# Moving the second probability tile of each attention step to GpSimd, in an attention and mixture-of-experts kernel

## The chip, the cores and the metric

The kernel runs on one core of one Trainium2 chip. The metric is the device time of one execution in microseconds (us). The five engines that matter here are TensorE (PE in the profile; PEld is its weight load), VectorE (DVE), ScalarE (ACT), GpSimd (POOL) and SyncE (SP), whose queue issues all DMAs of this kernel.

## The reference, cut to what matters

```python
scores = scale * np.matmul(q, k.transpose(0, 1, 3, 2))        # B=4, H=8, S=576, D=64
scores = scores + bias.transpose(2, 0, 1)[None]               # bias from a small MLP over positions
scores = scores - np.max(scores, axis=-1, keepdims=True)
attn = np.exp(scores)
attn = attn / (np.sum(attn, axis=-1, keepdims=True) + 1e-09)
x = np.matmul(attn, v)                                        # then (B*S, H*D) = (2304, 512)
...
for e in range(E):                                            # E=8 experts, F=1024
    out += P[:, e:e+1] * (np.maximum(x @ w1[e], 0.0) @ w2[e])
```

P comes from a Sinkhorn normalisation of the gate's softmax. All matrix products run in float16; where an operand needs more precision it is split into a float16 value (hi) and the float16 remainder (lo), and the products are summed.

## The kernel before

The program has two parts. The first (to about 490 us) computes the position bias, the attention, and as filler a large part of expert 0; the second runs the experts on what the attention left. The change touches the first part alone.

Work of the attention is cut by unit (16 units: a batch and a pair of heads) and step. A unit has five steps: four of two tiles (128 query rows x 576 keys each) and one of a single tile that holds the last 64 rows of both heads. That is 80 steps, 64 of them with two tiles, and 144 tiles. A step goes through these functions:

- `scores` (L897): PE writes the raw scores into one of two PSUM tiles `s`.
- `st_max` (L921): one custom VectorE instruction per tile adds the bias (tiles `br`, `br4`, `bt`), takes the row maximum into `st` and writes the result as float32 to `sb` (six buffers). The order listing calls it ISA, the profile CUSTOM_DVE_ANT_0.
- `st_exp` (L939): ScalarE takes the exponential in place in `sb`, with the row sum into `st`.
- `st_rcp` (L946): VectorE makes the reciprocal of the sum, a TENSOR_SCALAR and a RECIPROCAL on `st`.
- `st_hi` (L955): ScalarE multiplies `sb` by the reciprocal and rounds to float16, the first half of tile `ah` (two buffers; every third step in the middle units uses a part of `xc`).
- `st_lo` (L968): VectorE forms the remainder, `sb` times the reciprocal minus hi, as float16 in the second half of `ah` (SCALAR_TENSOR_TENSOR). Then one DMA, issued by SP, transposes the step's whole `ah` into `aT` (three buffers).
- `attend` (L982): PE multiplies `aT` by the split values `vs` into PSUM tile `pv`, two steps (LAG, L1105) after the step that completed the group.

Once per unit the queries and keys are split (`u_cut`, tile `qk`: ScalarE hi, VectorE lo), transposed on PE and copied out (`u_trans`, tile `qkT`), and the values split (`u_v`, tile `vs`). GpSimd has five copies per unit to do (`pairs`, L720: two of `qkT`, three of `vs`), and nothing else in this stretch apart from some copies of the bias.

From step 13 on, pieces of expert 0 (`run_piece`, L867; matmuls into tile `l`, evacuations to `area` and `ys`) are marked `later` and fill PE between the steps.

All of this is first recorded: class `Plan` holds each operation with its engine, a cost from `Engine.cost` (L226), and its dependencies, and `emit` (L130) replays it on a model of the engines and so fixes the order of every engine's queue, SP's included, before the kernel runs. Semaphores then enforce dependencies; each engine runs its own queue strictly in order. The line of nearly all instructions of this part is therefore that of the recorder, L210, and they are told apart by their tiles.

Of the kernel before, what the change touches and what calls it, by code (L numbers as in the profile page):

```python
# [12 lines left out]
AF = mybir.ActivationFunctionType  # L13
ALU = mybir.AluOpType
# [5 lines left out]
B, H, S, D = 4, 8, 576, 64  # L20
# [22 lines left out]
class Plan:  # L43
# [14 lines left out]
    def record(self, eng, cost, fn, ins, outs, move=None):  # L58
        g = self.group
        if g is not None:  # L60
            g[0] = eng
            g[1] += cost
            g[2].append(fn)
            for new, l in ((ins, g[3]), (outs, g[4])):
                l.extend(r for r in map(region, new) if r not in l)
            return
        self.node(eng, cost, fn, [region(x) for x in ins], [region(x) for x in outs], move)

    def node(self, eng, cost, fn, ins, outs, move=None):
        i, deps = len(self.nodes), set()  # L70
        cut = lambda a, b: a[0] < b[1] and b[0] < a[1]
        within = lambda a, b: b[0] <= a[0] and a[1] <= b[1]
        for t, p, f in ins:
            deps.update(j for w, q, g, j in self.seen.get(t, ()) if w and cut(p, q) and cut(f, g))
        for t, p, f in outs:
            l = self.seen.setdefault(t, [])
            deps.update(j for _, q, g, j in l if cut(p, q) and cut(f, g))
            l[:] = [x for x in l if not (within(x[1], p) and within(x[2], f))]
        for w, l in ((False, ins), (True, outs)):
            for t, p, f in l:  # L80
                self.seen.setdefault(t, []).append((w, p, f, i))
        deps.discard(i)
        self.nodes.append((eng, cost, fn, deps, self.prio, 0.0, move))
# [105 lines left out]
class Engine:  # L189
# [36 lines left out]
    def cost(self, op, out, ins):  # L226

        n = max(x.free_size() for x in [out] + ins)
        columns = sum(x.free_size() == 1 for x in ins)
        if self.name == "pe":  # L230
            c = 4 if ins[0].dtype == F32 else 1
            if out.partition_size() > 64:
                return c * max(64, out.free_size()) / 2350
            return c * max(82, out.free_size()) / 3500
        if self.name == "act":
            return (0.13 if ins and ins[0].space == PSUM else 0.16) + 0.03 * columns + n * 0.00097
        if self.name == "pool":
            return 0.15 + n * 0.0016
        if op == "tensor_copy" and ins[0].dtype == out.dtype == F16:
            return 0.06 + n * 0.00027  # L240
        if n <= 2:
            return 0.08
        return 0.12 + n * (0.0012 if ins[0].space != PSUM else 0.00112)
# [27 lines left out]
def attention_sinkhorn_moe(ctx, tc, q, k, v, w1, b1, w2, wg, m1, m2, xm, xm4, xf, sel, out):  # L271
# [12 lines left out]
    vec, act, pool, pe, sync = (  # L284
        Engine(plan, e, n)
        for e, n in ((nc.vector, "dve"), (nc.scalar, "act"), (nc.gpsimd, "pool"), (nc.tensor, "pe"), (nc.sync, "dma"))
    )
# [125 lines left out]
    with ExitStack() as actx:  # L413
# [105 lines left out]
        for kind in range(1, 4):  # L519
            vec.scalar_tensor_tensor(  # L520
                out=wr,
                in0=wbs[:, kind // 2, kind % 2, :],
                scalar=selt[:, kind : kind + 1],
                in1=wr,
                op0=ALU.mult,
                op1=ALU.add,
# [3 lines left out]
            out=wa.rearrange("p g (j k) -> p (g j) k", j=4),  # L530
            in0=wr.unsqueeze(1).broadcast_to([P, 16, HID]),
            in1=selt[:, 8:24].unsqueeze(2).broadcast_to([P, 16, HID]),
            op=ALU.mult,
# [89 lines left out]
        def bias_step(between=()):  # L623
# [27 lines left out]
            out=w1r, in0=pw[:, H : H + 2], scalar1=s_wb[:, 0:1], scalar2=2.0**-11, op0=ALU.mult, op1=ALU.mult  # L651
# [5 lines left out]
            out=w2m,  # L657
            in0=w2r.unsqueeze(2).broadcast_to([P, H, 4]),
            in1=selt[:, 4:8].unsqueeze(1).broadcast_to([P, H, 4]),
            op=ALU.mult,  # L660
# [19 lines left out]
        for i in range(2):  # L680
            r = slice(32 * i, 32 * i + 1)
# [110 lines left out]
        for n in range(8):  # L792
            for m in (2 * n, 2 * n + 1):
                nm, _, i = qk_order[m]
# [9 lines left out]
        with plan.urgent():  # L804
# [6 lines left out]
            out=c8, in0=u_qk[:, 0:1], scalar=0.125, in1=u_qk[:, 1:2], op0=ALU.mult, op1=ALU.mult  # L811
# [7 lines left out]
            out=g, in0=g0, scalar=s_qk[:, 0:1], in1=s_qk[:, 1:2], op0=ALU.mult, op1=ALU.mult  # L819
# [135 lines left out]
        def st_hi(s):  # L955

            n, u = len(s["sb"]), s["key"][0]
            if NHP <= u < 3 * NHP:
                ahs[0] += 1
            if ahs[0] % 3 == 2 and u < 3 * NHP:  # L960
                ah = xc[:, 1, : 4 * S].rearrange("p (i s) -> p i s", i=2)
            else:
                ah = wrk.tile([P, 2, 2 * S], F16, name="ah", tag="ah", bufs=2)
            s["ah"] = ah[:, :n]
            for i, sb in enumerate(s["sb"]):
                act.activation(s["ah"][:, i, 0:S], sb, AF.Copy, scale=s["st"][:, 3, i : i + 1])

        def st_lo(s):  # L968
            n, ah = len(s["sb"]), s["ah"]
            s["aT"] = wrk.tile([P, 9 * n, P], F16, name="aT", tag="aT" if n == 2 else "aT4", bufs=3 if n == 2 else 1)  # L970
            for i, sb in enumerate(s["sb"]):
                vec.scalar_tensor_tensor(
                    out=ah[:, i, S:],
                    in0=sb,
                    scalar=s["st"][:, 3, i : i + 1],
                    in1=ah[:, i, 0:S],
                    op0=ALU.mult,
                    op1=ALU.subtract,
                )
            sync.dma_start_transpose(out=s["aT"], in_=ah.rearrange("p n s -> p (n s)"))  # L980
# [161 lines left out]
        for n in range(NS + LAG + 1):  # L1142
# [19 lines left out]
            if 0 < n <= NS:  # L1162
                s = steps[n - 1]
                st_hi(s)
                st_lo(s)
                u, gi, hh = s["key"]
                groups.setdefault((u, gi), []).append(s)
                if gi == 2 or hh == 1:
                    due.append((n + LAG, u, gi, groups.pop((u, gi))))
# [21 lines left out]
        vec, act, pool, pe, sync = nc.vector, nc.scalar, nc.gpsimd, nc.tensor, nc.sync  # L1191
# [693 lines left out]
    for n, (e, b) in enumerate(seq):  # L1885
        r = visit[n]
        i, at_end, leaves = (b, r % 2), n % 5 == 4, visit[n + 1 : n + 2] != [r]
# [96 lines left out]
```

## Time and profile before

| | us |
|---|---|
| median of three timed runs | 1766.91 |
| lowest and highest of them | 1764.6, 1772.89 |
| profiled execution, first to last instruction (span) | 1765.7 |
| busy in that span: PE, DVE, ACT, POOL | 1681.9, 1427.0, 1086.1, 73.9 |

No time beside the span is listed for the profiled execution itself; its span lies inside the spread of the three runs, 1.2 us below their median. In the profile a busy PE is modelled and not a PE at its peak, and consecutive instructions of VectorE and ScalarE overlap a little, so the length of a row of two is less than twice that of one.

### The profile page before, as it was taken

The page shows a single profiled execution, that of the slowest core. Times are in us where ns is not written, and L with a number is a line of the kernel's source. Part 1 is how long each engine was busy: PE and PEld are TensorE (multiplying, and loading weights), DVE is VectorE, ACT ScalarE, POOL GpSimd, SP SyncE. Part 2 cuts the span into 40 slices and gives each one's busy share as a digit, 9 for nine tenths or more (in the row PEclk, how much of TensorE's full clock was granted, in tenths as well). Part 3 has the DMA queues.
Part 4 walks back from the last instruction along what each step waited for, and adds up shares of the span by engine and source line. Part 5 has one row for each costly group of instructions (what it writes and reads, how often), then busy time and mean ns, then how long its engine had stood idle before and what let it go on. Part 6 is the DMA issues. An engine that isn't in the chain of part 4 may idle for free.

```text
span 1765.7 us, 40391 instructions
## 1 busy us (share of the span) xinstructions
PE 1681.9 (95%) x16640; PEld 1374.4 (78%) x16640; DVE 1427.0 (81%) x2603; ACT 1086.1 (62%) x1930; POOL 73.9 (4%) x119
## 2 busy tenths in 40 slices
PE   7887897989999899999999999999999999999998
PEld 4554564656585688788988898889888988898887
DVE  6998989988866988678878887888788878876666
ACT  7997888888864766445554654565555644453443
POOL 0111011111002000000000000000000000000000
PEclk9998898999999999999999999999999999999999
DMA  7779899999974346545574456455654743463321
GB/s 259 245 174 241 184 211 210 216 191 210 187 236 167 120 176 215 173 142 184 179 264 151 156 203 239 158 176 194 206 189 168 253 178 132 166 236 103 103 77 37
DMA packets 290813, 322.52 MB, mean 183 GB/s; under 512 B 182972, under 2 KB 217284, under 8 KB 285636
## 3 DMA queue, kind: packets, MB, share of 16 engines
q1 hardware_dynamic: 290628, 319.94, 60.4%
q8 instruction: 130, 2.13, 0.5%
q14 instruction: 55, 0.45, 0.1%
HBM read 189.33 MB, written 88.08 MB: 157 GB/s over the span
## 4 chain that ended last, share of the span: by engine, by line
PE 82%; DVE 7%; DMA 5%; ACT 3%; issue 2%; SPq 0%; POOL 0%; DVEq 0%; ACTq 0%; POOLq 0%
PE bankA L1606 18%; PE bankA L1626 14%; PE bankB L1626 9%; PE bankE L1626 9%; PE bankE L1606 9%; PE l L210 7%; PE bankB L1606 4%; PE s L210 4%; PE pv L210 4%; PE bankA L393 2%; DMA aT<-ah 2%; ACT area L210 1%; DVE area L210 1%; DVE ah L210 1%; DVE sb L210 1%
## 5 line engine op out<-in xcount | busy, mean ns | idle before, releaser
L1606 PEld LDWEIGHTS <-slot 128*128 128x128 f16 x5040 | 451.6, 98 | 51.9 <-issue 5.3
L1626 PEld LDWEIGHTS <-hA 128*128 128x128 f16 x2268 | 221.3, 98 | 26.3 <-DVE hA L1219 0.4
L210 PEld LDWEIGHTS <-area 128*128 128x128 f16 (+1 forms) x2477 | 153.1, 100 | 99.5 <-issue 31.4
L1606 PE MATMUL bankE<-xt,slot 128*128 128x256 f16 (+1 forms) x1680 | 186.1, 262 | 2.0 <-DVE c L1219 2.0
L1651 ACT ACTIVATE hA<-c 128x512 f16<-128x512 f32 x189 | 118.3, 627 | 112.4 <-DVE c L1219 111.4
L1606 PE MATMUL bankA<-xt,slot 128*128 128x256 f16 (+1 forms) x1680 | 187.4, 263 | 0.0
L1626 PEld LDWEIGHTS <-hS 128*128 128x128 f16 x1512 | 148.0, 98 | 24.5 <-ACT hS L1651 4.5
L1626 PEld LDWEIGHTS <-area 128*128 128x128 f16 x1512 | 148.7, 98 | 21.7 <-issue 3.5
L1219 DVE SCALAR_TENSOR_TENSOR hA<-c,hA 128x512 f16<-128x512 f32 x189 | 127.4, 684 | 13.3 <-ACT hA L1651 11.1
L1710 ACT COPY u<-bankA 128x512 f32<-128x512 f32 (+1 forms) x70 | 37.8, 540 | 156.5 <-PE bankA L1626 156.5
L1663 ACT ACTIVATE u<-bankA 128x512 f32<-128x512 f32 x126 | 75.1, 596 | 72.0 <-PE bankA L1606 64.1
L210 PE MATMUL l<-area 128*128 128x512 f16 (+1 forms) x413 | 110.8, 385 | 5.5 <-ACT area L210 1.7
L210 ACT ACTIVATE sb<-sb,st 128x576 f32<-128x576 f32 x144 | 110.7, 771 | 7.9 <-DVE st L210 7.7
L1219 DVE SCALAR_TENSOR_TENSOR acc<-c,fs,acc 128x256 f32<-128x256 f32 x252 | 110.3, 479 | 2.0
L210 DVE SCALAR_TENSOR_TENSOR ah<-sb,st,ah 128x576 f16<-128x576 f32 x121 | 97.6, 831 | 15.7 <-ACT ah L210 15.7
L210 PE MATMUL s<-qkT 128*128 128x512 f16 (+3 forms) x560 | 83.3, 298 | 14.7 <-DVE st L210 14.1
L210 ACT ACTIVATE ah<-sb,st 128x576 f16<-128x576 f32 x121 | 89.5, 772 | 10.0 <-DMA aT<-ah 7.3
L1626 PE MATMUL bankA<-area,hS 128*128 128x256 f16 x756 | 89.9, 275 | 4.4 <-ACT hS L1651 3.9
L1626 PE MATMUL bankB<-area 128*128 128x256 f16 x756 | 90.1, 276 | 2.0 <-DVE area L1219 2.0
L1626 PE MATMUL bankA<-area 128*128 128x256 f16 x756 | 88.2, 273 | 1.0 <-ACT u L1710 1.0
L1626 PE MATMUL bankE<-area,hS 128*128 128x256 f16 x756 | 88.9, 273 | 0.1
L1626 PE MATMUL bankB<-area,hA 128*128 128x256 f16 x756 | 88.4, 273 | 0.2 <-DVE hA L1219 0.2
(242 smaller groups left out, 3163.4 us busy)
## 6 DMA issues: line engine op xcount, KB each, us to landing
sc_w<-stage SPq DMA_DIRECT2D x84, 512.0 KB
acc<-sc_y SPq DMA_DIRECT2D x102, 256.0 KB
area<-sc_w SPq DMA_DIRECT2D x48, 512.0 KB
sc_y<-acc SPq DMA_DIRECT2D x84, 256.0 KB
xt<-sc_t SPq DMA_DIRECT2D x18, 1024.0 KB
slot<-sc_w SPq DMA_DIRECT2D x36, 512.0 KB
bt<-sc_bias SPq DMA_DIRECT2D x26, 576.0 KB
raw<-in_moe_w_dram SPq DMA_DIRECT2D x28, 512.0 KB
```

Source lines behind the costliest of these rows:

```text
L210: self.plan.record(self.name, cost, lambda: fn(*args, **kw), ins, outs, move)
L393: pe.matmul(ps[:, :512], h[a][:, ft, j * P : (j + 1) * P], w[:, wl, c : c + 512], start=(ft == 0 and i == 0), stop=(ft == 7 and i == 2),)
L1219: vec.scalar_tensor_tensor(out=o, in0=x, scalar=s, in1=y, op0=op0, op1=op1)
L1606: pe.matmul(ps[:, jf * w : jf * w + w], t[:, a, c * 512 + f * P : c * 512 + f * P + P], x(xp, c), start=(first and jf == 0 and c == 0 and ...
L1626: pe.matmul(ps[:, j * 256 : j * 256 + 256], h[:, a, fc * w + j * P : fc * w + j * P + P], t[:, wp, fc * 256 : fc * 256 + 256], start=(firs ...
L1651: on_act(0.58, lambda: act.activation(h[:, 0, sl], x, AF.Relu if relu else AF.Copy), [r], wk)
L1663: on_act(0.55, lambda: act.activation(tmp[k], bank[b], f, scale=HS), [b], [k], 0)
L1710: on_act(0.27 * nt, lambda: act.copy(tmp[k][:, :n], bank[b][:, :n]), [b], [k], 0)
```

## The change

Of the two tiles of a step the first (i = 0) is treated as before. For the second, GpSimd multiplies `sb` by the reciprocal in place, ScalarE rounds the product into hi without a scale, and GpSimd subtracts hi from `sb` to form lo. The single tile of a one-tile step is treated as a first tile. The planner's cost of a GpSimd operation with two tile inputs becomes 0.3 + 0.0022 per column; the one for one input stays.

```diff
         if self.name == "pool":
-            return 0.15 + n * 0.0016
+            return 0.15 + n * 0.0016 if len(ins) - columns < 2 else 0.3 + n * 0.0022
...
             for i, sb in enumerate(s["sb"]):
-                act.activation(s["ah"][:, i, 0:S], sb, AF.Copy, scale=s["st"][:, 3, i : i + 1])
+                r = s["st"][:, 3, i : i + 1]
+                if i:
+                    pool.tensor_scalar(out=sb, in0=sb, scalar1=r, scalar2=1.0, op0=ALU.mult, op1=ALU.mult)
+                    act.copy(s["ah"][:, i, 0:S], sb)
+                else:
+                    act.activation(s["ah"][:, i, 0:S], sb, AF.Copy, scale=r)
...
             for i, sb in enumerate(s["sb"]):
+                if i:
+                    pool.tensor_tensor(out=ah[:, i, S:], in0=sb, in1=ah[:, i, 0:S], op=ALU.subtract)
+                    continue
                 vec.scalar_tensor_tensor(
                     out=ah[:, i, S:],
```

The planner makes the order anew. Three places show how, all of them in the same stretch: the step whose reciprocal stands in `st_132` (called A below; tiles `sb_133`, `sb_134`) and the next one, `st_135` (B; `sb_136`, `sb_137`), in a unit whose keys go to `qkT_129` and values to `vs_147`.

VectorE, from the reciprocal of B on, before:

```order
L210 RECIPROCAL st_135<-st_135 128x2
L210 SCALAR_TENSOR_TENSOR ah_144<-sb_133,st_132,ah_144 128x576
L210 SCALAR_TENSOR_TENSOR ah_144<-sb_134,st_132,ah_144 128x576
L210 ISA sb_133,st_143<-s_119,bt_124,sms 128x576
L210 ISA st_143 128x1
L210 ISA sb_134,st_143<-s_117,bt_124,sms 128x576
```

and with the change:

```order
L210 RECIPROCAL st_135<-st_135 128x2
L210 SCALAR_TENSOR_TENSOR ah_144<-sb_133,st_132,ah_144 128x576
L210 ISA sb_133,st_143<-s_119,bt_124,sms 128x576
L210 ISA st_143 128x1
L210 ISA sb_134,st_143<-s_117,bt_124,sms 128x576
```

The remainder of A's second tile has left VectorE's queue; the maxima of a later step follow one place sooner.

ScalarE, the two roundings of step A, with what each instruction waits for, before:

```order
L210 COPY qkT_129<-l_0_113 128x1024 [waits Pool_49]
L210 CAST area<-l_1_115 128x512 [waits Activation_49]
L210 ACTIVATE ah_144<-sb_133,st_132 128x576 [waits DMAHW7_49,DVE_49]
L210 ACTIVATE ah_144<-sb_134,st_132 128x576
L210 ACTIVATE xc<-pv_112 128x256 [waits PE_49]
```

and with the change:

```order
L210 ACTIVATE l_1_115<-l_1_115 128x512 [waits PE_49]
L210 ACTIVATE ah_144<-sb_133,st_132 128x576 [waits DMAHW7_49,DVE_49,Activation_49]
L210 CAST area<-l_1_115 128x512 [waits Activation_49]
L210 CAST ah_144<-sb_134 128x576 [waits Pool_49]
L210 ACTIVATE sb_140,st_139<-sb_140,st_139 128x576
```

The second rounding, which followed the first without a wait, is now a CAST that waits for GpSimd, with another instruction put between the two.

GpSimd in this stretch, before (copies of two units):

```order
L210 COPY vs_145<-vs_145 64x320
L210 COPY vs_145<-vs_145 64x2x128
L210 COPY vs_145<-vs_145 64x2x32
L210 COPY qkT_129<-qkT_129 64x576 x2
L210 COPY vs_147<-vs_147 64x320
```

and with the change:

```order
L210 TENSOR_SCALAR sb_134<-sb_134,st_132 128x576 [waits DVE_49,Activation_49]
L210 TENSOR_SCALAR sb_137<-sb_137,st_135 128x576 [waits DVE_49,Activation_49]
L210 TENSOR_TENSOR ah_144<-sb_134,ah_144 128x576 [waits DMAHW0_49,Activation_49]
L210 TENSOR_SCALAR sb_141<-sb_141,st_139 128x576 [waits DVE_49,Activation_49]
L210 COPY qkT_129<-qkT_129 64x576 [waits Activation_49,Pool_49]
L210 COPY qkT_129<-qkT_129 64x576
L210 TENSOR_TENSOR ah_142<-sb_137,ah_142 128x576 [waits DMAHW3_49,Activation_49,Pool_49]
L210 COPY vs_147<-vs_147 64x320 [waits PE_49,Activation_49,Pool_49]
```

Between the copies of `qkT` and `vs` now stand the two operations of each step. The product of B is queued ahead of the remainder of A, and the two copies of keys ahead of the remainder of B.

## Rows read from the trace of the kernel before

**Rows 1.** Busy time by stretch: bias with first steps, weights' stretch, steady attention.

```profile
core 0: us, PE busy (x) PEld busy (x) DVE busy (x) ACT busy (x) POOL busy (x), PEclk, DMA share, GB/s
60.00:150.00 90.00, 77.53 (x1084) 48.79 (x1084) 82.75 (x168) 80.51 (x160) 17.94 (x28) 0.96 0.72 187
150.00:200.00 50.00, 34.27 (x281) 20.30 (x278) 47.53 (x109) 37.85 (x71) 2.23 (x7) 0.76 1.02 238
200.00:490.00 290.00, 268.09 (x2664) 172.44 (x2664) 250.29 (x579) 244.41 (x500) 37.83 (x57) 0.96 0.99 200
```

**Rows 2.** Chain of waits by line, first of 150 to 205 us, then 205 to 490 us.

```profile
by line: DMA aT<-ah 15.3%; DVE ah L210 13.2%; DVE area L210 10.1%; issue 9.3%; PE s L210 9.0%; PE pv L210 8.4%; DVE sb L210 6.3%; PE l L210 5.7%; DVE sms L210 5.3%; DVE st L210 2.9%; ACT sb L210 2.8%; DVE qk L210 2.6%; ACT ys L210 2.4%; DMA
...
by line: PE l L210 39.1%; PE pv L210 17.7%; PE s L210 13.0%; DMA aT<-ah 6.6%; issue 4.9%; DMA aT<-xc 3.7%; DVE ah L210 3.6%; DVE sb L210 3.5%; DVE qk L210 1.4%; ACT ah L210 1.1%; DMA vnat<-in_v_dram 1.1%; DVE area L210 0.7%; DVE xc L210 0.7
```

**Rows 3.** Waits of PE, 200 to 490 us: total us, times, longest.

```profile
PE s L210 <- DVE st L210: 8.9, 12, 1.7
PE pv L210 <- DMA aT<-ah: 4.7, 5, 2.0
PE l L210 <- DVE qk L210: 2.8, 1, 2.8
PE pv L210 <- DMA aT<-xc: 2.7, 2, 2.3
```

**Rows 4.** VectorE's instructions on tile st: ns min/median/max, first and last start.

```profile
L210 DVE SCALAR_TENSOR_TENSOR ah<-sb,st,ah x121: 796/812/1252, 86.3 to 486.4; 128x576 f16<-128x576 f32 x121
L210 DVE TENSOR_SCALAR st<-st x80: 130/158/644, 79.8 to 478.6; 128x2 f32<-128x2 f32 x64, 128x1 f32<-128x1 f32 x16
...
L210 DVE SCALAR_TENSOR_TENSOR xc<-sb,st,xc x23: 798/814/1219, 229.9 to 393.2; 128x576 f16<-128x576 f32 x23
```

**Rows 5.** VectorE, 60 to 200 us: the remainders there (count, busy us, mean ns).

```profile
L210 DVE SCALAR_TENSOR_TENSOR ah<-sb,st,ah 128x576 f16<-128x576 f32 x28 | 23.0, 834 | 0.0
```

**Rows 6.** Groups of ScalarE: count, busy us, mean ns, idle before.

```profile
L210 ACT ACTIVATE ah<-sb,st 128x576 f16<-128x576 f32 x121 | 89.5, 772 | 10.0 <-DMA aT<-ah 7.3
...
L1531 ACT ACTIVATE stage<-raw,fs 128x1024 f16<-128x1024 f32 x42 | 48.0, 1143 | 15.3 <-DMA sc_w<-stage 9.9 <-DVE fs L1507 4.5 <-DVE raw L1540 0.9
...
L1404 ACT CAST xt<-c 128x512 f16<-128x512 f32 x6 | 3.6, 621 | 3.3 <-DVE c L1410 3.3
```

**Rows 7.** GpSimd's instructions, by tile or by form: ns min/median/max or mean.

```profile
L210 POOL COPY qkT<-qkT x24: 662/663/1201, 212.7 to 454.2; 64x576 uint32<-64x576 uint32 x24
...
L1298 POOL TENSOR_TENSOR lg<-lg,fs x8: 433/560/1260, 518.6 to 572.9; 128x144 f32<-128x144 f32 x8
...
masks.py:199 POOL TENSOR_SCALAR_AFFINE_SELECT ident<-ident x1: 292/292/292, 1.0 to 1.0; 128x128 f32<-128x128 f32 x1
...
L1977 POOL MEMSET const-float32-0.0<- 128x1 f32 x1 | 0.1, 98 | 0.2 <-issue 0.2
```

**Rows 8.** Timeline, VectorE beside GpSimd at two moments: start us, us, instruction.

```profile
213.30 2.35 DVE L210 SCALAR_TENSOR_TENSOR ah<-sb,st,ah 128x576 f16<-128x576 f32 x2
...
212.71 2.33 POOL L210 COPY qkT<-qkT 64x576 uint32<-64x576 uint32 x2 [21.39 <-ACT qkT L210]
...
228.45 0.81 DVE L210 CUSTOM_DVE_ANT_0 sb<-s,bt,sms 128x576 f32<-128x576 f32 x1
...
227.85 1.39 POOL L210 COPY qkT<-qkT 64x576 uint32<-64x576 uint32 x2 [12.81 <-ACT qkT L210]
```

**Rows 9.** Timeline of steps A and B, the place of the order listings.

```profile
311.58 0.16 DVE L210 RECIPROCAL st<-st 128x2 f32<-128x2 f32 x1
...
312.84 0.17 DVE L210 RECIPROCAL st<-st 128x2 f32<-128x2 f32 x1
312.93 1.54 DVE L210 SCALAR_TENSOR_TENSOR ah<-sb,st,ah 128x576 f16<-128x576 f32 x2
...
318.97 1.95 DVE L210 SCALAR_TENSOR_TENSOR ah<-sb,st,ah 128x576 f16<-128x576 f32 x2 [0.54 <-ACT ah L210]
...
318.39 1.92 POOL L210 COPY qkT<-qkT 64x576 uint32<-64x576 uint32 x2 [17.69 <-ACT qkT L210]
```

## The prediction

> **What bounds the kernel now.** I read the busy time by stretch first, because the change lies wholly in the first part of the program. Up to 200 us VectorE is the fullest engine: 82.8 of 90 us, then 47.5 of 50 us, while TensorE has gaps [rows 1]. From 200 to 490 us TensorE leads with 268 of 290 us, but VectorE (250) and ScalarE (244) are close behind, and GpSimd does 38 [rows 1]. GpSimd is nearly empty and VectorE full, which is the case for the change.
>
> Next, the chain of waits. Between 150 and 205 us about 40% of it is VectorE's (13.2% on `ah` alone), and TensorE's granted clock averages 0.76. From 205 us on 70% is TensorE's own (l, pv, s), about 10% the transposing DMA into `aT`, and 9% VectorE's [rows 1, 2]. So in the long stretch a lighter VectorE can give back only what TensorE waits for it: 8.9 us for maxima that free a score tile, and 2.8 us once for `qk` [rows 3]. Against that TensorE already waits 7.4 us, in seven places, for transposes [rows 3], and these come after the very instruction that moves.
>
> **The change part by part.** It touches one tile in each of the 64 two-tile steps, the count being that of the reciprocals on 128x2 [rows 4].
>
> *Removed from VectorE:* 64 remainders. One alone takes 0.81 us [rows 4], two in a row 1.54 [rows 9], so I count 0.77 each: 49 us. 28 remainders lie before 200 us [rows 5], so 14 of the removed ones do, 11 us; the other 50, 38 us, lie where TensorE leads.
>
> *On ScalarE* the second rounding loses its scale operand. With it: 0.772 us at 576 columns and 1.143 at 1024, thus 0.83 ns a column; without it 0.621 at 512, thus 0.67 at 576 [rows 6]. 64 x 0.10 = 6 us less. I count nothing for it: ScalarE's busy time is covered by TensorE's in the long stretch and by VectorE's before. Without that cover it would be a gain of 6 us.
>
> *Added on GpSimd:* neither operation stands in this trace. For the product the nearest rows are the one-input copy of 576 columns, 0.66 us, as the lower end, and the select at 128 columns, 0.292 us. With the 0.098 us of a one-column memset as the fixed part, the select gives 1.5 ns a column and 0.97 us at 576, the upper end [rows 7]. I take 0.8, since the product reads like the copy and computes like the select. For the two-input subtraction the fastest 128x144 one took 0.433 us. (0.433 - 0.098)/144 is 2.3 ns a column, thus 1.44 us, which I take because only this row has two inputs. The ends are the copy's 0.66, were the second input free, and four times 0.433, 1.73. Per step 2.24 us (1.3 to 2.7), over 64 steps 143 us (85 to 173) on an engine that was busy 58 us of these 430.
>
> [...]
>
> *Contention between the two.* Two remainders take 1.54 us undisturbed and 2.35 beside two GpSimd copies; the copies took 2.33 there, but 1.39 beside a maximum, which itself kept its 0.81 [rows 8, 9]. So GpSimd and those VectorE operations that read both inputs from SBUF hold each other up, and those that read PSUM (maxima, evacuations) don't. The small TENSOR_SCALAR of the reciprocal is hit too: median 0.158 us, longest 0.644 [rows 4]. Per added GpSimd operation VectorE then loses between nothing and its whole length.
>
> [...]
>
> *What a step looks like.* At A the reciprocal ended at 311.74 us and the last remainder at 314.47 [rows 9]. With the change the product of A runs to 312.6 beside maxima, and the rounding ends near 313.3. Then the product of B is next in GpSimd's queue. It needs B's reciprocal (313.01) and finds VectorE in the first remainder until about 313.7, so it ends at 314.5, and A's subtraction ends at 315.95: the transpose starts 1.5 us later than before. At B the remainders ended at 320.92; the two key copies held GpSimd to 320.31 [rows 9], the subtraction follows and ends near 321.75, 0.8 us later. VectorE loses nothing at A and 0.3 to 1.4 us at B, where its splitting of the values meets the subtraction. I take 0.4 us of new VectorE waits per step.
>
> *What waits behind.* The second rounding now waits for GpSimd, and behind it ScalarE's queue holds the exponentials of the next step. SP's queue holds later loads behind the transpose. `sb` and `ah` come free 1 to 2 us later; with about 60 steps in the 290 us, so 5 us a step, and two or more buffers I count nothing for that. If it fails, ScalarE's exponentials are late next.
>
> *The sum,* against the profiled span of 1765.7 us, which is 1.2 us under the median of the runs. VectorE: -49 + 64 x 0.4 = -23 us net, of it -5 before 200 us and -18 after. Before 200 us the chain is VectorE's for about 40%, thus -2 us (all of 11 us at most). After, 18 of 250 us is 7% of VectorE; I take a third of TensorE's 8.9 us of waits for it, -3 us (11.7 at most). The seven waits for transposes would each grow by up to 1.2 us, the mean of A and B; since the planner placed the matmuls of `pv` anew, I take half: +4 us (up to +15 if as many others come over their threshold). Together -1 us: **1765 us** on the median's basis, no change. Half a per cent, 8.8 us, is about what a measurement of this kernel can tell from none.
>
> **The rivals.**
>
> *VectorE is really relieved.* GpSimd's turns fall mostly beside maxima and evacuations. For it: the maxima, undisturbed, alone take 0.81 us per tile [rows 8], 117 us over 144 tiles. Then all 11 us before 200 us and the 11.7 us of TensorE's waits come back: 1766.9 - 22.5 = 1744 us, with anything to 1757 in this case. Against it: TensorE's work doesn't shrink. Chance 0.32.
>
> *GpSimd's queue is late (slower).* Its order is fixed by the planner, which knows nothing of the contention. A subtraction stands behind the product of the next step, and two key copies with three value copies stand between others. Where the reciprocal ahead comes late, the subtraction slips by a step, about 5 us. The group's `pv` is placed two steps, some 9 us, after its last step, and the transpose lies between, so this decides once a subtraction ends some 4 us later than the remainder did. At one such place in each of the 16 units, with 1.5 us lost on TensorE each, 24 us: 1790 us. For it: TensorE's existing waits show no slack in seven places [rows 3]. Against: at A and B I find only 0.8 to 1.5 us. Chance 0.22.
>
> *The turns cost VectorE more than it saves.* With 1.5 us of waits a step it is busy 380 - 49 + 96 = 427 of 430 us [rows 1] and bounds both stretches: about 25 to 40 us slower, 1792 to 1807. For it: the remainder's 1.25 us at worst [rows 4]. Against: the maxima keep their 0.81 us [rows 8], and at A I find no loss. Chance 0.08.
>
> [...]
>
> **How the numbers follow.** No change (1758 to 1776) 0.38, relieved 0.32, late queue 0.22, costly turns 0.08. Faster 0.32, same 0.38, slower 0.30. The range runs from the full relief, 1744, to the late queue's price, 1790; below and above I leave out less than 2 in 10.
>
> **What the profile after would show.** The subtraction near 1.4 us at its fastest and the product near 0.8, both with long tails; GpSimd busy near 200 us; VectorE busy 20 to 30 us less, its remaining remainders well over 0.81 us on average; the rounding at 0.67. Longer waits of `pv` for `aT`, shorter ones of `s` for `st`. I would be wrong if the attention ended more than 9 us from its place near 490 us: earlier with VectorE's waits for GpSimd small, or later with ScalarE or TensorE idle behind GpSimd.

## The result and the profile after

The change is slower. The median of four runs is 1783.47 us (1780.96 to 1786.62) against 1767.64 us (1764.6 to 1772.89) for four runs of the kernel before; the ratio is 1.011 with a 95% interval of 1.0089 to 1.0131. The profiled execution has a span of 1779.1 us against 1765.7.

Busy time by stretch of the changed kernel, the same three stretches as [rows 1], with the same columns:

```profile
60.00:150.00 90.00, 76.97 (x1055) 48.86 (x1055) 77.77 (x155) 75.69 (x151) 24.90 (x31) 0.91 0.67 180
150.00:200.00 50.00, 31.07 (x270) 18.60 (x265) 45.94 (x97) 34.67 (x68) 23.92 (x25) 0.73 0.85 203
200.00:490.00 290.00, 259.89 (x2561) 167.05 (x2558) 230.59 (x523) 236.54 (x491) 148.20 (x158) 0.95 0.95 198
```

VectorE is busy 354.3 us of these 430, where it was 380.6. Yet TensorE did less in the same time: 259.9 us instead of 268.1 in the long stretch, 31.1 instead of 34.3 before it, at a lower granted clock (0.95 for 0.96 and 0.73 for 0.76). The work left over went behind 490 us, so a fixed window flatters the change. For the same work the window must reach to the last matmul into `pv`, 495.7 us before and 515.3 us with the change:

```profile
0.00:495.70 495.70, 433.38 (x4769) 274.73 (x4770) 426.39 (x938) 412.26 (x822) 59.80 (x103) 0.95 0.92 212
0.00:515.30 515.30, 437.71 (x4767) 278.31 (x4768) 408.38 (x874) 407.10 (x822) 205.60 (x231) 0.93 0.87 204
```

VectorE, with 64 instructions fewer, is busy 18.0 us less; the prediction had 23. The attention ends 19.6 us later: TensorE's nearly equal number of matmuls takes 4.3 us more, at a mean granted clock of 0.93 instead of 0.95, and TensorE stands idle 15.3 us longer. The span grows by only 13.4 us, so the second part is some 6 us shorter; no experiment looks into that.

Instructions on the tiles `ah`, `sb` and `qk`: ns min/median/max, first and last start, forms.

```profile
L210 POOL TENSOR_SCALAR sb<-sb,st x64: 737/749/1347, 82.9 to 496.8; 128x576 f32<-128x576 f32 x64
L210 POOL TENSOR_TENSOR ah<-sb,ah x54: 1270/1282/2246, 86.3 to 503.2; 128x576 f16<-128x576 f32 x54
L210 ACT CAST ah<-sb x54: 655/667/705, 85.5 to 502.5; 128x576 f16<-128x576 f32 x54
L210 DVE SCALAR_TENSOR_TENSOR ah<-sb,st,ah x67: 792/819/1916, 87.1 to 507.5; 128x576 f16<-128x576 f32 x67
L210 DVE SCALAR_TENSOR_TENSOR qk<-nat,sms,qk x32: 803/810/1836, 60.7 to 455.4; 128x576 f16<-128x576 f32 x32
```

The product takes 0.75 us at the median, the subtraction 1.28, the rounding 0.67. VectorE's remaining remainders on `ah` kept their median (0.81 [rows 4], now 0.82), but the longest rose from 1.25 [rows 4] to 1.92 us, and the remainder of the queries and keys (`qk`) reached 1.84. Single instructions are held up by nearly one whole subtraction: the longest remainder, at 291.33 us, began with a subtraction of 1.28 us (291.35) and took 1.10 us more than the median; that of `qk`, at 221.72, met one of 1.77 us (from 221.17) and took 1.03 us more.

Waits of PE from 200 to 490 us, as in [rows 3]:

```profile
PE s L210 <- DVE st L210: 15.5, 14, 2.2
PE l L210 <- DVE qk L210: 2.7, 2, 2.5
PE pv L210 <- DMA aT<-xc: 2.3, 2, 1.2
PE pv L210 <- DMA aT<-ah: 2.0, 2, 1.2
```

TensorE waits 15.5 us for maxima where it waited 8.9, so that wait grew although VectorE has less to do. Its waits for transposes, which the prediction saw growing, fell from 7.4 to 4.3 us.

The chain of waits of the changed kernel can be followed back only to 289.6 us, so here it is from 290 to 490 us, first of before and then of the change:

```profile
by line: PE l L210 39.8%; PE pv L210 18.0%; PE s L210 12.6%; DMA aT<-ah 6.6%; DMA aT<-xc 5.3%; issue 3.7%; DVE ah L210 3.2%; DVE sb L210 2.9%; DMA vnat<-in_v_dram 1.5%; ACT ah L210 1.2%; DVE xc L210 0.9%; DVE qk L210 0.8%; DVE st L210 0.6%;
by line: PE l L210 34.6%; PE pv L210 17.9%; PE s L210 12.1%; DMA aT<-ah 8.9%; DMA aT<-xc 6.6%; issue 4.1%; DVE sb L210 3.5%; DVE ah L210 2.7%; ACT ah L210 1.8%; POOL ah L210 1.3%; DVE st L210 1.2%; POOL sb L210 1.2%; DVE area L210 1.0%; DVE
```

TensorE's own share (l, pv, s) falls from 70 to 65%, and the transposes' rises from 12 to 15.5%.

### The profile page after: what moved, and what is told of

The parts are those of the page before. It is cut to its first block, busy times and chain, and to the rows that moved or that the text cites. A ratio compares the mean times of both kernels' runs of the same rounds, so it can differ in the third digit from the quotient of the medians.

```text
span 1779.1 us, 40628 instructions
## 1 busy us (share of the span) xinstructions
PE 1682.4 (95%) x16640; PEld 1376.3 (77%) x16640; DVE 1409.7 (79%) x2539; ACT 1081.4 (61%) x1930; POOL 219.7 (12%) x247
## 4 chain that ended last, share of the span: by engine, by line
PE 75%; DMA 3%; DVE 3%; ACT 2%; issue 1%; POOL 0%; SPq 0%; DVEq 0%; ACTq 0%; POOLq 0%
PE bankA L1614 18%; PE bankA L1634 13%; PE bankE L1634 9%; PE bankE L1614 9%; PE bankB L1634 9%; PE bankB L1614 5%; PE l L210 4%; PE pv L210 2%; PE bankA L393 2%; PE s L210 1%; DMA aT<-ah 1%; PE bankB L374 1%; DMA aT<-xc 1%; PE bankE L374 1%; PE bankS L1449 1%
## 5 line engine op out<-in xcount | busy, mean ns | idle before, releaser
L1634 PE MATMUL bankA<-area,hA 128*128 128x256 f16 x756 | 88.3, 273 | 0.0
L1634 PE MATMUL bankE<-area,hA 128*128 128x256 f16 x756 | 88.3, 273 | 0.0
```

The lines of the kernel that those rows point to most:

```text
L1634: pe.matmul(ps[:, j * 256 : j * 256 + 256], h[:, a, fc * w + j * P : fc * w + j * P + P], t[:, wp, fc * 256 : fc * 256 + 256], start=(firs ...
```

## The experiments

Ratios are to the kernel before, run beside each kernel on the same chip, with the 95% interval in brackets; 0.1% is 1.8 us. The first theory was the **port** (VectorE and GpSimd hold each other up), its rival the **chain** (the remainder comes later in each step). A third came up on the way: the planner's **new order**.

### Parts of the change, each with an order made anew

**e1**, no work for GpSimd:

```diff
-                    pool.tensor_tensor(out=ah[:, i, S:], in0=sb, in1=ah[:, i, 0:S], op=ALU.subtract)
+                    vec.tensor_copy(ah[:, i, S:], ah[:, i, 0:S])
```

with the rounding as before.

> This kernel leaves GpSimd out: hi of the second tile is formed by ScalarE with its scale as before the change, and the remainder is not computed at all; VectorE copies hi (float16, about 0.2 us) into its place. So VectorE is relieved of about 64 x 0.6 = 37 us and nothing else changes. Port theory (GpSimd and VectorE hold each other up) and chain theory (three operations in a row on two engines in place of two make every transpose later) both expect faster than before, by 5 to 20 us (1747 to 1762). A theory that the planner's new order, with VectorE's load gone, is itself bad expects about the time of the change, 1780.

Measured 1.0029 (1.0018 to 1.0040): a lighter VectorE and a slower kernel. The copy takes 0.30 us at the median. In this row of its busy time by stretch VectorE is at 222.6 us instead of 250.3 [rows 1], and TensorE did 265.2 instead of 268.1:

```profile
200.00:490.00 290.00, 265.17 (x2646) 170.83 (x2643) 222.64 (x577) 242.68 (x498) 37.56 (x60) 0.97 0.97 199
```

So neither port nor chain can be all of it; nor did a new order alone bring the 1780 us that its theory had.

**e2**, the subtraction alone on GpSimd (the rounding keeps its scale, no product):

> ScalarE scales and rounds the second tile as before the change; GpSimd only subtracts hi from the tile, which is not normalised (so the remainder is not the reference's). 64 products of 0.75 us and ScalarE's wait for them are gone; the 1.28 us subtractions stay. Chain theory: most of the loss is gone, 1765 to 1772. Port theory: GpSimd's share falls by a third, so does the loss: 1776 to 1780.

Measured 1.0095 (1.0072 to 1.0117), close to the whole change and in the port theory's range: without the product nearly all of the loss is there. How much of it is the new order this run can't tell.

**e3**, the product on GpSimd, the subtraction (`vec.tensor_tensor`) on VectorE:

> GpSimd normalises the second tile and ScalarE rounds it as in the change, but VectorE forms the remainder by a subtraction, as before on its own engine. GpSimd's added work is 64 x 0.75 us, VectorE's load is that of before. Chain theory: ScalarE's wait for the product stays, the slow subtraction goes, half of the loss stays, 1770 to 1778. Port theory: a third of the contention and no relief: 1770 to 1775.

Measured 1.0006 (0.9988 to 1.0024): no difference, where both theories had a loss. The product costs nothing here, although its mean rose from 0.93 us in the change to 1.14.

**e7**, GpSimd forms hi of the second tile as float16, VectorE its remainder; ScalarE is relieved of 64 roundings:

> Another division: GpSimd forms hi of the second tile itself (one product, written as float16), VectorE forms the remainder as before the change; ScalarE is relieved of 64 x 0.77 = 49 us. e3_product_only showed that 64 products cost about nothing. If ScalarE's place in the chain is what holds the engines (VectorE waits for its hi 15 to 23 us in the runs so far), faster by 5 to 20 us, 1743 to 1758. If nothing but TensorE and the transposes bounds the attention, about the time of before, 1758 to 1767.

Measured 1.0015 (0.9999 to 1.0030). ScalarE fell from 244.4 to 216.7 us between 200 and 490 us, and nothing came of it, as the prediction had it for ScalarE's 6 us.

### Idle work and plain writes on GpSimd

**e5**, the kernel before with 64 added subtractions on GpSimd, for whose results nobody waits:

```diff
+            if n == 2:
+                sb = s["sb"][1]
+                pool.tensor_tensor(out=sb, in0=sb, in1=ah[:, 1, 0:S], op=ALU.subtract)
             sync.dma_start_transpose(out=s["aT"], in_=ah
```

> The kernel before, with 64 subtractions of the change's size added on GpSimd that nothing waits for: each starts once the second tile's remainder is formed, reads that tile and hi, and writes the tile in place (its buffer comes free a little later, as in the change). The chain from the reciprocal to the transpose is that of before. Port theory: VectorE's two-input instructions are held up by some 12 us more in total and the kernel is 8 to 16 us slower, 1771 to 1779. Chain theory: within 0.3% of before, 1759 to 1768.

Measured 1.0046 (1.0027 to 1.0064), at the lower edge of what the port theory had and beyond the chain theory's 0.3%, though its interval reaches below that: with idle work on GpSimd the kernel is 8 us slower. But the planner was shown the 64 operations and made a new order here too (the queues of TensorE, VectorE and ScalarE all differ from before), so the 8 us are not the port's alone. In this row of its windows the same VectorE instructions are busy 265.6 us instead of 250.3:

```profile
200.00:490.00 290.00, 263.05 (x2603) 168.00 (x2603) 265.59 (x578) 244.28 (x498) 104.79 (x108) 0.96 0.95 196
```

**e4**, the change with two memsets (0.577 us each) in place of the subtraction, so that GpSimd writes and reads nothing there, and **e6**, the same with three memsets of the remainder's place, meant as a chain 1.15 us longer:

```diff
-                    pool.tensor_tensor(out=ah[:, i, S:], in0=sb, in1=ah[:, i, 0:S], op=ALU.subtract)
+                    pool.memset(sb, 0.0)
+                    pool.memset(ah[:, i, S:], 0.0)
```

> As the change, but GpSimd's subtraction is replaced by two memsets of about the same total length: one on the normalised tile (it waits for ScalarE's rounding, as the subtraction did) and one on the remainder's place (the remainder is left out, zero). They write and read nothing. The length of the chain, the queue and VectorE's load stay; of the contention the part that comes from GpSimd's reads goes. Port theory: VectorE's remainders are back near 0.81 us on average and most of the loss is gone, 1765 to 1772. Chain theory: the time stays near the change's, 1779 to 1785.

> As e4_write_only, but with three memsets in place of one on the remainder's place, so that GpSimd's part of the chain is 1.15 us longer and the transposes start at least as late as with the change; still nothing in it reads. Remainder left out as there. Port theory: at most 4 us over e4_write_only, 1768 to 1773. Chain theory: back to the loss of the change, 1778 to 1786.

Measured 1.0037 (1.0023 to 1.0051) and 1.0051 (1.0030 to 1.0072). Without the subtraction two thirds of the loss are gone. But these two runs do not part port from chain, for the expectations have the chain wrong. Nothing makes a memset of the remainder's place wait for the rounding, and the planner put these memsets ahead of it, as soon as a buffer `ah` was free; in e6 the first starts at 2.5 us, before any step:

```profile
L210 POOL MEMSET ah<- x162: 569/578/1185, 2.5 to 491.7; 128x576 f16 x162
```

From the reciprocal of a two-tile step to the issue of its transpose (80 reciprocals on `st` and 80 transposes, paired in order of time; the means of the 64) it takes 7.02 us before, 8.69 with the change, but 6.67 in e4 and 6.94 in e6. So e4 removed the reads and the late transposes together, and e6 lengthened the chain by 0.3 us, not by 1.15. What e1 and e4 share, 0.3 to 0.4%, was still unexplained: both have a new order.

### Order and instructions apart

In the next three the planner is shown one set of instructions and another goes out in its places, so that order and work change apart. In short, for the remainder (`then` replaces what is issued, not what is planned):

```diff
+                def lo(sb=sb, out=ah[:, i, S:], hi=ah[:, i, 0:S]):
+                    pool.real.tensor_tensor(out=out, in0=sb, in1=hi, op=ALU.subtract)
                 vec.scalar_tensor_tensor(
...
                     op1=ALU.subtract,
+                    then=lo if i else None,
```

**e8**, order of before, VectorE relieved by the copy of e1; **e11**, order of before, instructions of the change; **e12**, order of the change, instructions of before:

> The kernel before, in which VectorE copies hi into the remainder's place in the second tile of each step (the remainder of the second tile is left out of the computation); the planner is given the old cost and the old dependencies, so that every engine's queue has the order of before. VectorE has about 0.5 us x 64 = 32 us less to do. If the 0.29% of e1 is the planner's new order and the relief itself gives something: 1753 to 1760 us on a basis of 1762.5 to 1767 for the kernel before. If the relief is worth nothing whatever the order: within 0.1% of the kernel before, neither faster nor slower, and the order then owns the 0.29% of e1. If a lighter VectorE itself harms: 0.2 to 0.3% slower as in e1.

> The change's instructions in the order of before: the planner is shown the old instructions (costs and dependencies), and what goes out in the place of the second tile's rounding is the product on GpSimd and the rounding, and in the place of its remainder the subtraction on GpSimd. All of the change's work and waits, none of its new order. Order theory (the new order costs some 0.6%, as between e1 and e8, the instructions 0.5%): 0.2 to 0.6% slower than before. Port and chain theory (the loss belongs to the instructions): 0.9 to 1.5% slower, more than the change since the planner did not know of the longer chain.

> The instructions of before in the order of the change: the planner is shown the change's operations, and what goes out is the old rounding on ScalarE and the old remainder on VectorE, in the place where the planner put the subtraction. No GpSimd work is added and VectorE is not relieved. Order theory: 0.5 to 1.0% slower than before, though nothing but the order differs. Port and chain theory: 0 to 0.4% slower.

Measured: e8 0.9969 (0.9953 to 0.9985), e11 1.0061 (1.0041 to 1.0081), e12 1.0056 (1.0040 to 1.0071). Port and chain have neither e11 nor e12; the order theory, which for e11 left the instructions a share, has e8 and e12 and misses e11 by 0.01%. **The loss has two nearly equal parts.** The new order alone costs 0.56%, with not one instruction exchanged; the instructions alone cost 0.61%; together 1.17%, and the change lost 1.1%. Other pairs with the same instructions in a new and an old order agree on the order's price: e1 over e8 0.60%, e2 over e14 (below) 0.56%, the change over e11 0.49%. The relief is worth 0.3% in the old order, which the new order took away in e1.

The row of the maxima with `br`, the last of which is the last maximum of all, shows where each kernel ends its attention (ns min/median/max, first and last start), for the kernel before, the change, e12 and e11 in turn:

```profile
L210 DVE CUSTOM_DVE_ANT_0 sb<-s,br,sms x80: 795/807/819, 67.2 to 476.9; 128x576 f32<-128x576 f32 x80
```

```profile
L210 DVE CUSTOM_DVE_ANT_0 sb<-s,br,sms x80: 792/810/820, 68.0 to 495.4; 128x576 f32<-128x576 f32 x80
```

```profile
L211 DVE CUSTOM_DVE_ANT_0 sb<-s,br,sms x80: 790/809/819, 68.8 to 486.9; 128x576 f32<-128x576 f32 x80
```

```profile
L211 DVE CUSTOM_DVE_ANT_0 sb<-s,br,sms x80: 791/806/819, 70.3 to 489.0; 128x576 f32<-128x576 f32 x80
```

The last maximum comes 18.5 us later with the change, 10.0 with its order alone, 12.1 with its instructions alone. The two losses arise at different places. The 28th of the 144 maxima starts at 186.6 us before, at 195.5 with the change, at 194.3 in e12 and at 190.4 in e11 (timeline of VectorE): the order's loss is there almost whole by 195 us, that of the instructions grows to the end. The windows of e12 before 200 us show TensorE's clock down:

```profile
60.00:150.00 90.00, 78.13 (x1066) 49.24 (x1064) 79.67 (x161) 76.27 (x152) 13.61 (x21) 0.91 0.67 180
150.00:200.00 50.00, 32.96 (x273) 19.38 (x267) 47.22 (x107) 36.10 (x69) 5.60 (x11) 0.69 0.89 216
```

The granted clock is 0.91 and 0.69 where it was 0.96 and 0.76 [rows 1], though GpSimd does nothing new. One such place is near 110 us, here in e12:

```profile
102.00:108.00 6.00, 4.29 (x44) 2.09 (x44) 5.96 (x15) 5.46 (x10) 1.49 (x3) 0.95 0.54 161
108.00:114.00 6.00, 4.16 (x40) 2.47 (x39) 5.32 (x10) 1.66 (x4) 1.47 (x3) 0.50 0.78 162
```

TensorE is busy 4.29 of the first 6 us, where it was 5.55 before, and in the next 6 the granted clock is 0.50; before, it was 1.00 in both.

### What in the instructions costs

**e14**, order of before with the subtraction alone on GpSimd; **e15**, order of before with two memsets in its place:

> The order of before; only the subtraction goes to GpSimd, of the tile that was not normalised (so the remainder of the second tile is wrong); ScalarE scales and rounds as before, and no product is added. The chain of a step is some 0.5 to 0.8 us longer than before instead of some 1.5. Port theory (what costs is the subtraction beside VectorE's instructions): 0.45 to 0.7% slower, nearly as e11. Chain theory (what costs is the later remainder and the rounding that waits): 0 to 0.3%.

> As e14, but two memsets of the same places (1.15 us together, in place of the subtraction's 1.28) stand for the subtraction: GpSimd only writes, and the remainder of the second tile is left out of the computation (zero). VectorE is relieved as in e8. Port theory: 0.3% faster to 0.1% slower. Chain theory: as e14, within 0.15%.

Measured 1.0039 (1.0025 to 1.0054) and 0.9975 (0.9963 to 0.9988). e14 falls between the two ranges, just under the port theory's; e15 is where the port theory had it, and far from where the chain theory had it. Here both memsets come after the rounding in GpSimd's queue. The two kernels have the same order in every other queue and operations of nearly the same length in the chain (1.28 and 1.15 us; from reciprocal to transpose 7.17 and 6.95 us at the mean), and differ by 0.64%, 11 us: that is the price of the subtraction, which reads two tiles, over the memsets, which read none. Against e8 (6.62 us) e15's transposes come 0.3 us later, and the time differs by 0.06%, within the intervals; so a chain some tenths of a us longer costs next to nothing. The 1.7 us of the change itself were not tried alone. Windows and VectorE's remainders, e14:

```profile
200.00:490.00 290.00, 262.73 (x2618) 167.37 (x2618) 234.81 (x528) 244.60 (x499) 105.82 (x108) 0.96 0.93 197
```

```profile
L211 DVE SCALAR_TENSOR_TENSOR ah<-sb,st,ah x67: 796/817/1924, 87.5 to 493.1; 128x576 f16<-128x576 f32 x67
```

and e15:

```profile
200.00:490.00 290.00, 269.48 (x2748) 174.74 (x2747) 213.93 (x526) 245.12 (x501) 88.58 (x159) 0.98 0.97 205
```

```profile
L211 DVE SCALAR_TENSOR_TENSOR ah<-sb,st,ah x67: 797/816/1221, 87.5 to 479.8; 128x576 f16<-128x576 f32 x67
```

The longest remainder falls from 1.92 to 1.22 us. In the same 290 us TensorE issued 130 matmuls fewer beside the subtraction, at a clock of 0.96 instead of 0.98. For the same work, to the last `pv`, e14 and then e15:

```profile
0.00:502.10 502.10, 433.49 (x4769) 274.85 (x4770) 406.94 (x874) 412.51 (x823) 143.90 (x167) 0.95 0.90 209
0.00:489.30 489.30, 427.84 (x4769) 272.12 (x4770) 382.21 (x874) 411.83 (x823) 124.03 (x231) 0.96 0.92 215
```

The same 874 instructions of VectorE take 406.9 us beside the subtraction and 382.2 beside the memsets. Of these 24.7 us more, the sums of the durations give 12.6 to the remainders on `ah` and `xc`, 8.7 to the splits of queries, keys and values, and 1.9 to the small TENSOR_SCALAR of the reciprocal; the maxima are unchanged (the longest 0.82 us in both). The same 4769 matmuls take 5.7 us more and TensorE is idle 7.2 us longer; from 60 us on it waits 23.2 us for maxima instead of 19.2. So about half of the delay shows as waits and about half as matmuls at a lower mean clock (0.95 for 0.96).

The rest of e11's loss, 0.22% over e14, is the product with the rounding that waits for it; the intervals of the two overlap, so its size is uncertain.

### Where and why the order costs

**e9**, the change planned with GpSimd's costs set to the means of its own trace:

> The change, with the planner's costs of the two new GpSimd operations set to the means measured in the changed kernel (0.93 us for the product, 1.37 for the subtraction, in place of 1.07 and 1.57), so that the whole order is made anew. Port and chain theory (the loss belongs to the instructions, not to one order): 0.9 to 1.3% slower than before, as the change. If a large part of the loss is one bad order made from wrong costs: 0.2 to 0.7%.

Measured 1.0097 (1.0081 to 1.0112): one more order, nearly the same loss. Better costs for the new operations don't mend it.

**e10**, the change in units 0 to 3 alone, and **e16**, in units 4 to 15 alone (`if i and s["key"][0] < 4:` and `>= 4`):

> The change in units 0 to 3 alone (16 of the 64 two-tile steps), those of the stretch up to some 200 us, where VectorE was the fullest engine; units 4 to 15 as before. The prediction's reading (there VectorE bounds, so its relief comes back): 2 to 11 us faster, 0.1 to 0.6%. Loss spread evenly over the steps: a quarter of 1.1%, 0.3% slower. Loss only where TensorE leads: 0.0%.

> The change in units 4 to 15 alone (48 of the 64 two-tile steps); up to some 200 us every queue has the order and the instructions of before, from there on the order is new. If the order's share (0.56%) arises in the first four units, as the traces of e10 and e12 suggest, and the instructions' share (0.61%) is even over the steps: three quarters of 0.61, 0.3 to 0.6% slower. If the new order costs as much in the steady part: 0.8 to 1.0%. If the first four units hold nearly all of the loss: 0 to 0.3%.

Measured 1.0073 (1.0053 to 1.0093) and 1.0065 (1.0050 to 1.0081). A quarter of the steps brings 0.73%, more than any of the three readings, and exactly where VectorE was fullest and the prediction saw a gain. The other 48 steps bring 0.65%, just over the range for an even share of the instructions' cost. Three quarters of e11's 0.61% are 0.46%, so some 0.2% of the order's loss may lie behind 200 us too; the two runs together are 1.38%, more than the change's 1.1%, and a finer split isn't to be had from these intervals.

**e13**, the change with one split put back: ScalarE's rounding and, with it, VectorE's part. In the change its rounding of the values of unit 1 stands ahead of an exponential and waits for a load (start us, us, instruction, idle before it):

```profile
110.77 0.83 ACT L210 ACTIVATE vs<-vnat,sms 128x640 f16<-128x640 f32 x1 [2.64 <-DMA vnat<-in_v_dram]
111.69 0.78 ACT L210 ACTIVATE sb<-sb,st 128x576 f32<-128x576 f32 x1
```

```diff
-        for _, i in sorted(order):
+        at = {i: t + self.push.get(i, 0.0) for t, i in order}
...
+            if u == 1:
+                plan.push[len(plan.nodes)] = 6.0
```

> The change with one place of its order put back: ScalarE's rounding of the values of unit 1 (vs from vnat), which stands ahead of two exponentials and waits for a load at 108 to 111 us there, goes seven places later, behind those (as in the order of before), and VectorE's part of that split four places later. All else as in the change. If the order's share of the loss (0.5% of 1.1%) hangs on this wait, after which TensorE's granted clock was 0.5: 0.5 to 0.9% slower than before. If it is spread over many places: 1.0 to 1.2%, as the change.

Measured 1.0115 (1.0096 to 1.0134): nothing came back. Its row at the same place tells why:

```profile
112.25 0.78 ACT L213 ACTIVATE sb<-sb,st 128x576 f32<-128x576 f32 x1 [3.56 <-DVE st L213]
```

With the load's wait gone the exponential waits 3.56 us for its own maximum and starts no sooner (at 105.5 us in the kernel before). The load only hid it. The order of VectorE's queue shows what has come ahead of this maximum (`sb_133`). Rows of before, in part:

```
RECIPROCAL sms<-sms 128x1
SCALAR_TENSOR_TENSOR ah_144<-sb_137,st_135,ah_144 128x576
TENSOR_TENSOR aT_0_118<-s_117,area 128x512
ISA sb_133,st_143<-s_119,br_109,sms 128x576
...
SCALAR_TENSOR_TENSOR qk_126<-nat_120,sms,qk_126 128x9x64
SCALAR_TENSOR_TENSOR area<-s_117,sms,aT_0_118 128x8x32
SCALAR_TENSOR_TENSOR vs_145<-vnat_116,sms,vs_145 128x640
```

and of the change:

```
SCALAR_TENSOR_TENSOR qk_126<-nat_120,sms,qk_126 128x9x64
...
SCALAR_TENSOR_TENSOR qk_126<-nat_121,sms,qk_126 128x9x64
...
SCALAR_TENSOR_TENSOR vs_145<-vnat_116,sms,vs_145 128x640
...
SCALAR_TENSOR_TENSOR ah_142<-sb_140,st_139,ah_142 128x576
...
ISA sb_133,st_143<-s_119,br_109,sms 128x576
```

The remainder of `sb_137` has left this queue, and the planner put other work there: one split of queries, one of keys and one of values, 0.8 to 0.9 us each, and a later remainder now stand ahead of the maximum that used to precede most of them. In the trace of the change GpSimd adds to it at this place: the remainder starts at 107.56 us, beside a subtraction that started at 107.31, and takes 1.64 us. How much of the order's 0.56% hangs on this one place wasn't tried. That the freed room is what let the other work in is read from the order and not shown by a run. In e12 as a whole, to the last `pv` at 505.8 us, TensorE is busy 437.8 us, 4.4 more than before, and idle 5.7 us longer.

## Why the prediction was wrong

It said no change, 1765.0 us, and the kernel got slower by 1.1%. That 1783.47 lies inside the range of 1744 to 1790 is luck: the upper end was the price of a late queue, which isn't what happened. Its own sum, 1 us less than the median of 1766.9, gives 1766 and not 1765; nothing hangs on that.

**Right:** the prices of the operations (0.8 taken and 0.75 measured for the product, 1.44 and 1.28 for the subtraction, 0.67 and 0.67 for the rounding), ScalarE's relief at nothing (e7), and the kind and even the size of the contention: 0.4 us of waits a step were taken, and e14 has 24.7 us over 64 steps more than e15, 0.39 a step. VectorE's net was put at 23 us less and came out at 18.0.

**Wrong, first step:** "VectorE: -49 + 64 x 0.4 = -23 us net". The two were netted against each other as if a microsecond taken away and one put on were worth the same. They are not. From the kernel before to e15 VectorE's busy time to the last `pv` fell by 44.2 us (426.4 to 382.2) and the kernel won 0.25%, 4.4 us: a tenth. From e15 to e14 it rose by 24.7 us and the kernel lost 11.3 us: nearly half. By these rates the removed remainder was off the path most of the time. The waits fall on remainders, splits and small instructions that stand ahead of maxima in VectorE's queue; TensorE waits longer for those maxima (23.2 us in e14, 19.2 in e15), and its clock is lower (0.95 for 0.96). At the rates measured, 49 us of relief are 5 us and 26 us of waits are 12, and the net is a loss of 7; with the new order's 10 us (below) that is 17, where the medians differ by 15.8 and the ratio gives 19. In the sum's own terms: the 3 us of TensorE's waits for maxima that were to come back became 6.6 us more (8.9 to 15.5).

**Wrong, second step:** the planner's new order was counted only by the matmuls of `pv` ("I take half: +4 us"). It costs 0.56%, 10 us, with the instructions of before (e12), and not by `pv`: the waits for transposes fell. The 4 us for transposes became 3.1 us less (7.4 to 4.3). The gain of 2 us put before 200 us was on the very place where the change loses most: the 28th maximum comes 8.9 us late, and the change in the first four units alone brings 0.73% (e10).

**The rivals.** The late queue had the side and nearly the time, 1790, but not the mechanism: the transposes do come 1.7 us later at the mean, but TensorE's waits for `aT` shrank, and of those 1.7 us the new order alone, with the old instructions, brings 1.2 (e12, 8.20 us from reciprocal to transpose). What the late transposes cost beside that stays open: their share of the chain rose, and ScalarE waits 10.8 us for a free `ah` where it waited 7.3 [rows 6]. The costly turns had the mechanism of one half and overpriced it, since VectorE, busy 230.6 of 290 us in the long stretch, never came near bounding both. The real relief exists, and is worth 0.3% (e8), not the 1.3% of 1744 us. The sign named for a wrong forecast came: the last maximum, and with it the end of the attention, is 18 to 20 us late.

None of these kernels that computes the whole result is faster than the kernel before.

## What to carry to other kernels

Price a microsecond taken off a full engine and one put on it apart: here what was taken off lay mostly off the path, and what was put on fell on whatever stood in the queue, also ahead of what the bound engine waits for. Where a planner fixes all queues, a change is two changes, its instructions and a new order; run the new instructions in the old order and the old ones in the new order before either is blamed. Before a wait is removed as the cause, look at what its engine would wait for next. Before two kernels are compared in a fixed window, see whether the same work lies in it; and before a run is read as a longer chain, see in its trace whether the chain got longer.

## What was not expected of the hardware

GpSimd's own instructions are held up as well: the product's shortest is 0.737 us and the longest 1.35 in the change, and with the two-input subtraction on VectorE (e3) its mean is 1.14 us and its longest 1.88. A memset of 576 columns on GpSimd takes 0.577 us at the median for float32 and float16 alike in e4, with the longest at 0.60 in e15; the subtraction's 1.27 us reach 2.25 in the change. There is one exception: in e6 a single memset of 256 took 1.185 us, at 93.47 us, beside a one-input TENSOR_SCALAR of 1152 columns on VectorE that took 1.09 us instead of the 0.80 it takes at 109.52 us in the change.
